# Splitting the first token chunk of an attention front end in two halves, in a fused sketch-attention and MLP kernel on Trainium2

## The chip, the cores and the metric

The kernel runs on one core of one Trainium2 chip. It is timed as device microseconds of one execution, the median of five runs. A second source is one profiled execution, whose trace gives the start and duration of every instruction on the engines: PE (TensorE matmuls), PEld (TensorE weight loads), DVE (VectorE), ACT (ScalarE), POOL (GpSimd), and SP, which here only issues DMAs.

## The reference, cut to what matters

```python
def phi(x):                                   # 32 -> 64 features per token and head
    a = np.einsum('rd,bhsd->bhsr', S1, x)
    b = np.einsum('rd,bhsd->bhsr', S2, x)
    return np.einsum('bhsi,bhsj->bhsij', a, b).reshape(*x.shape[:-1], r * r)
q_p, k_p = (phi(q), phi(k))
kv = np.einsum('bhsf,bhsd->bhfd', k_p, v)
z = np.sum(k_p, axis=2)
num = np.einsum('bhsf,bhfd->bhsd', q_p, kv)
den = np.einsum('bhsf,bhf->bhs', q_p, z)[..., None] + 1e-06
x = num / den                                 # then (B, H, S, D) -> (B*S, H*D)
h = x @ w_in
out = (0.5 * h * (1.0 + erf(h / sqrt(2)))) @ w_out
```

There are 4 batches, 4 heads, 1088 tokens and 32 dimensions per head. `w_in` is 128 x 2048 and `w_out` 2048 x 128. S1, S2, `w_in` and `w_out` arrive as 64-bit floats, and the kernel itself turns them into 32-bit ones; the program calls that "rounding".

## The kernel before, in words

The tokens of each batch are 1024 "main" ones in two chunks of 512 and 64 "remaining" ones. That gives eight main chunks (n = 0 to 7) and a ninth of the remaining tokens of all batches. For each chunk the query features are multiplied with that batch's `kv` and `z`, divided, laid out as `xT` (128 model dimensions by 512 tokens), and fed to 16 hidden tiles (`hidden`, L591: matmul L596, Gelu L603) and their projections (L673 and L724).

Nothing of the MLP can start before batch 0 is summed over its keys and chunk 0 is divided. The text from L757 to L816 is this start, written out by hand. All engines run their instructions in the order of the text, and a dependency ties each instruction to the one before it on its engine (L992 to L998). So the order in the text is the order in each queue.

The start runs as follows. Three matmuls of noughts (`keep_busy`, L755) precede the key transposes (L333). The sketch matrices are transposed (`sketches`, L319). Keys go through the sketch (L375) and become features (L389 and L392); the queries of chunk 0 are expanded (L497, L504, L510). `kv_first` (L432) sums `kv` over eight token blocks for each of two head groups r. The remaining keys of batch 0 go their own way: `key_turn_rem` transposes them (L333 for PE, L335 for the copy on ACT), `key_features_rem` sketches them (L399 on PE, L404 on ACT, L405 on POOL), and `kv_first_rem` (L438) adds them to `kv`. ACT copies the sum out of PSUM as `kz` (L794). The queries of chunk 1 are transposed (L333, copy L796).

Then `attend_by_token` (L552) computes numerators and denominators of chunk 0 with tokens on partitions: 32 small matmuls (L562) into two PSUM banks, one per pair of heads. DVE adds 1e-6 to the denominators (L567, one instruction per bank), takes reciprocals (L568) and multiplies (L570, one per bank) into `x_tok`. `turn_x` (L573) transposes `x_tok` with four matmuls (L578) into two banks, and ACT and DVE copy one half each into `xT` (L581). After a further matmul of noughts (L810) the first hidden tile begins. Between these lie chunk 1's expansion (`expand_products(1)`), and the rounding of the first pieces of the weights: `low_words` L267 and `exponents` L279 on ACT, `fields` L271 and L273, `mantissas` L287 and `signs` L292 on DVE, `product` L297 on POOL or DVE.

The loads of `w_out` piece 0 (L784) and of everything else (`load_rest`, L801) are issued by SP, but each `w_out` load of the first two pieces waits for a one-element write by POOL (L168), which serves as a gate in time.

From L948 the steps are a fixed list: chunk 0 and chunk 1 each take hidden tiles 0 to 3, then the rest follow, with projections two steps behind. In step t = 3 chunk 1 goes through `attend_by_token` as well, and in step 4 through `turn_x`.

PSUM has eight banks here: two for hidden tiles (`h_ps`), two for outputs (`o_ps`), and two pairs for other work (`w_ps`). A pool hands out its buffers in turn, and who gets one waits for the last reader of what it held.

Of the kernel before, what the change touches and what calls it, by code (L numbers as in the profile page):

```python
# [16 lines left out]
def kernel(  # L17
# [49 lines left out]
    def work_banks():  # L67

        return wps.tile([128, 2, CW], FP, name="w_ps")
# [283 lines left out]
    def key_turn(b, r, ps, copy, midway=lambda: None):  # L353
        kT[r] = transposed(ps, "kT", [four_tokens("k", b, h, c) for h in (r, r + 2) for c in range(NCH)], copy, midway)
# [71 lines left out]
    def kv_first(ps, r, tokens=range(J)):  # L426

        for i in tokens:

            ch, t, one = i // 4, i // 2 % 2, i % 2  # L430
            for c in range(NP):
                pe.matmul(ps[c * F:(c + 1) * F, r * 2 * D:(r + 1) * 2 * D], lhsT=flat(k_p[0, r][:, t, c * 4 + ch * 2 + one]),  # L432
                          rhs=v_aug[r][:, c, i, :], start=(r == 0 and i == 0), stop=False, skip_group_check=True)
# [54 lines left out]
    def expand_products(n):  # L488


        W = width[n]
        B_of[n] = [work_banks() for i in range(2)]
        for s in range(2):
            for g in range(G):
                for c in range(NP):
                    rows = slice(g * D, (g + 1) * D)
                    pe.matmul(B_of[n][g // 2][c * F:(c + 1) * F, g % 2, s * W // 2:(s + 1) * W // 2],  # L497
                              lhsT=Srep[rows, s].rearrange("p i j -> p (i j)"),
                              rhs=qT[n][rows, 2 * c:2 * c + 2].rearrange("p r j t -> p r (j t)"), start=True, stop=True)
        qp[n] = att.tile([128, 2, CW], FP, name="q_pT")  # L500

    def expand_copy(n, i):
        A[i] = att.tile([128, 2, CW // 2], FP, name="A_sb")
        act.copy(out=A[i][:, :, :width[n] // 2], in_=B_of[n][i][:, :, :width[n] // 2])  # L504

    def expand_multiply(n, i):
        W = width[n]
        a, b = (t.rearrange("f g (r x) -> f g r x", r=2) for t in (A[i][:, :, :W // 2], B_of[n][i][:, :, W // 2:W]))
        if n < NMAIN:
            dve.tensor_mul(out=qp[n].rearrange("f r (g x) -> f g r x", g=G)[:, 2 * i:2 * i + 2], in0=a, in1=b)  # L510
            return

        cols = qp[n][:, :, :W].rearrange("f r (j g t) -> f g r j t", g=G, t=32)
        a, b = (x.rearrange("f g r (j t) -> f g r j t", t=32) for x in (a, b))
        for g in range(2):
            dve.tensor_mul(out=cols[:, 2 * i + g], in0=a[:, g], in1=b[:, g])
# [32 lines left out]

    x_tok = {}  # L550

    def attend_by_token(n, banks, meanwhile=lambda: None):  # L552

        x_tok[n] = att.tile([128, JC, H, D], FP, name="x_tok", bufs=1)
        den = att.tile([128, NP, JC * 2], FP, name="den_tok")
        for i in range(JC):
            for r in range(2):
                for half in range(2):
                    for c in range(NP):
                        rows, at, tok = slice(c * F, (c + 1) * F), (i * 2 + r) * C, i * 128 + half * 64  # L560
                        v_at = kz_cols(0, 2 * c + r)[0]
                        pe.matmul(banks[c][half * 64:(half + 1) * 64, at:at + C], lhsT=qp[n][rows, r, tok:tok + 64],  # L562
                                  rhs=kz[0][rows, v_at:v_at + C], start=True, stop=True)
        meanwhile()
        nd = [banks[c][:, :JC * 2 * C].rearrange("p (g c) -> p g c", c=C) for c in range(NP)]
        for c in range(NP):
            dve.tensor_scalar(out=den[:, c], in0=nd[c][:, :, D], scalar1=1e-6, scalar2=None, op0=AX.add)  # L567
        dve.reciprocal(out=den, in_=den)  # L568
        for c in range(NP):
            dve.tensor_mul(out=x_tok[n][:, :, 2 * c:2 * c + 2], in0=nd[c][:, :, 0:D].rearrange("p (j r) d -> p j r d", r=2),  # L570
                           in1=den[:, c].rearrange("p (j r) -> p j r", r=2)[:, :, :, None].broadcast_to([128, JC, 2, D]))

    def turn_x(n, banks):  # L573

        xT[n] = att.tile([128, CW], FP, name="xT", bufs=3)
        for i, ps in enumerate(banks):
            for j in range(2):
                pe.transpose(ps[:, j * 128:(j + 1) * 128], in_=x_tok[n][:, 2 * i + j].rearrange("p h d -> p (h d)"),  # L578
                             identity=ident)
        for i, (ps, copy) in enumerate(zip(banks, (by_act, by_dve))):  # L580
            copy(out=xT[n][:, i * 256:(i + 1) * 256], in_=ps[:, :256])  # L581


    g_of, o_of = {}, {}
# [1 line left out]
    def w_tile(w, fi):  # L586
        i = max(i for i, (c0, c1) in enumerate(pieces) if c0 <= fi * 128)
        at = fi * 128 - CUTS[i]
        return w[i][:, at:at + 128]

    def hidden(n, fi, by_halves=False):  # L591
        W = width[n]
        ps = hidden_bank()
        w = w_tile(w_in_sb, fi)
        for rows in (slice(0, 64), slice(64, 128)) if by_halves else (slice(0, 128),):
            pe.matmul(ps[rows, :W], lhsT=w[:, rows], rhs=xT[n][:, :W], start=True, stop=True)  # L596
        if n < NCH and fi < USUAL:
            g_of[n, fi] = mlp.tile([128, CW], FP, name="g", bufs=4)
        else:
            if fi % NB == 0:  # L600
                blocks[n, fi // NB] = block(FP)
            g_of[n, fi] = blocks[n, fi // NB][:, fi % NB]
        act.activation(out=g_of[n, fi][:, :W], in_=ps[:, :W], func=ACT.Gelu)  # L603

# [159 lines left out]
    r.signs()  # L764
    r.product_for_heads(SR_heads)
    key_turn(0, 0, hidden_bank(), by_act)
    sketches()
    key_turn(0, 1, hidden_bank(), by_act)
    query_turn(0)
# [7 lines left out]
    for i in range(2):  # L777
        query_features(0, i)
    kv_bank = out_bank()
    kv_first(kv_bank, 0)  # L780
    key_turn_rem(0, banks[1], by_act)
    kv_first(kv_bank, 1, range(J // 2))
    key_features_rem(0, banks[1], by_pool=True)
    load_w_out(0, gated=True)  # L784
    kv_first(kv_bank, 1, range(J // 2, J))
    kv_first_rem(kv_bank)
    w_in = [Rounding(w) for w in w_in_sb[:2]]
    w_out = [Rounding(w_out_sb[0], beside=w_in[0])]
    w_in[0].low_words()
    w_in[0].fields()  # L790
    w_in[0].exponents()
    late = []
    query_turn(1, lambda **a: late.append(a))
    act.copy(out=kz[0], in_=kv_bank[:, :128])  # L794
    w_in[1].low_words()
    by_act(**late[0])  # L796
    w_in[0].mantissas()
    w_in[0].signs()
    w_in[0].product(pool)
    w_in[1].fields()  # L800
    load_rest()  # L801
    w_out.append(Rounding(w_out_sb[1], beside=w_in[1]))
    w_in[1].exponents()
    banks = [hidden_bank(), hidden_bank()]
    attend_by_token(0, banks)
    expand_products(1)
    w_in[1].mantissas()
    expand_copy(1, 0)
    turn_x(0, [hidden_bank(), hidden_bank()])
    keep_busy(1, out_bank())  # L810
    w_in[1].signs()
    w_in[1].product(pool)
    expand_copy(1, 1)
# [134 lines left out]
    for t in range(len(steps) + LAG):  # L948
        if t < 4:

            hidden(0, t)
            if t == 1:
                w_out[0].exponents()
                w_out[0].low_words()
                w_out[0].finish()
                w_out[1].fields()
            if t == 2:
                w_out[1].low_words()
            if t == 3:
                attend_by_token(1, halves(work_banks()), lambda: (w_out[1].mantissas(by_pool=True),  # L960
                                                                  w_out[1].exponents()))
                w_out[1].signs()
                w_out[1].product()
                for u in range(4):
                    for f, *a in products[u]:
                        f(*a)
            continue
        if t == 4:
            turn_x(1, [work_bank(), work_bank()])
# [59 lines left out]
```

## Time and profile before

| | |
|---|---|
| median of 5 runs | 271.6 us (271.29 to 273.21) |
| the profiled execution's own time | 271.96 us |
| its span, first to last instruction | 270.1 us, so 1.86 us lie around it |
| PE busy | 264.5 us, 98% of the span |
| DVE, ACT, POOL busy | 153.2, 136.6 and 170.3 us |
| first hidden matmul of chunk 0 starts (L596) | 16.86 us |
| steady alternation of hidden tiles and projections | from about 25 us, one hidden tile or projection per 0.86 us |

How to read it: a matmul on 32-bit floats appears as two rows in the trace (four hidden tiles are "x8"), a transpose as one. Ends of matmuls are modelled, so that a stream of matmuls overlaps in the trace: the hidden matmul's row has 592 ns, but in the stream one starts every 430 ns. The view by slices shows PE at nine tenths in all but the first and the last slice; the first slice is 6.75 us wide, so what happens in the start has to be read in the timeline.

### The profile page before, as it was taken

How to read it: one execution, taken by the hardware profiler on the slowest of the kernel's cores; microseconds unless marked ns; L12 is line 12 of the kernel's file. 1: busy time of each engine (PE TensorE's matmuls, PEld its weight loads, DVE VectorE, ACT ScalarE, POOL GpSimd, SP SyncE). 2: the span in 40 equal slices, each digit the busy share in tenths (PEclk: the TensorE clock that was granted, in tenths of full speed). 3: DMA queues.
4: the chain of work that ended last, by engine and by line, in shares of the span. 5: the costliest groups of instructions: out<-in, count | busy, mean ns of one | idle time of the engine just before them, and what ended most of it. 6: DMA issues, size and time to landing. Idle time of an engine off the chain costs nothing.

```text
span 270.1 us, 6237 instructions
## 1 busy us (share of the span) xinstructions
PE 264.5 (98%) x2557; PEld 138.1 (51%) x2557; DVE 153.2 (57%) x242; ACT 136.6 (51%) x272; POOL 170.3 (63%) x178
## 2 busy tenths in 40 slices
PE   8999999999999999999999999999999999999994
PEld 6745445354445545435445445444544544445794
DVE  4856879514793699379214997287018901750140
ACT  4554777456625633573347433663357334733431
POOL 3512006899998498368865896668866886777300
PEclk9999999999999999999999999999999999999998
DMA  7479263626101000110200000100200020011020
GB/s 204 134 231 340 61 165 70 173 60 175 18 0 32 12 0 2 19 22 1 41 1 2 0 2 13 29 2 1 38 2 0 2 40 2 0 21 20 1 42 20
DMA packets 37869, 13.52 MB, mean 50 GB/s; under 512 B 28240, under 2 KB 37200, under 8 KB 37840
## 3 DMA queue, kind: packets, MB, share of 16 engines
q1 hardware_dynamic: 37648, 13.05, 19.1%
q8 instruction: 20, 0.33, 0.5%
q10 hardware_dynamic: 192, 0.07, 0.1%
q14 instruction: 9, 0.07, 0.1%
HBM read 10.88 MB, written 2.23 MB: 49 GB/s over the span
## 4 chain that ended last, share of the span: by engine, by line
PE 97%; DVE 1%; issue 0%; ACT 0%; POOL 0%
PE h_ps L596 44%; PE o_ps L673 32%; PE o_ps L724 5%; PE w_ps L497 3%; PE w_ps L721 3%; PE w_ps L537 2%; PE w_ps L444 2%; PE w_ps L755 1%; PE w_ps L375 1%; PE h_ps L333 1%; PE o_ps L432 1%; PE h_ps L562 0%; PE w_ps L562 0%; PE o_ps L333 0%; DVE x_tok L570 0%
## 5 line engine op out<-in xcount | busy, mean ns | idle before, releaser
L596 PE MATMUL h_ps<-xT,w_in 128*64 128x512 f32 (+3 forms) x518 | 140.8, 577 | 0.2 <-DVE xT L581 0.2
L603 ACT ACTIVATE block<-h_ps 128x512 f32<-128x512 f32 (+1 forms) x128 | 72.8, 571 | 101.6 <-PE h_ps L596 98.5
L673 PE MATMUL o_ps<-block,w_out 128*64 128x256 f32 x224 | 57.9, 381 | 0.0
L596 PEld LDWEIGHTS h_ps<-xT,w_in 128*64 128x64 f32 (+1 forms) x518 | 42.1, 143 | 29.6 <-issue 9.6
L638 POOL TENSOR_TENSOR bits_low<-block 128x512 f32<-128x512 f32 x28 | 36.5, 1303 | 27.7 <-ACT block L603 27.5
L673 PEld LDWEIGHTS o_ps<-block,w_out 128*64 128x64 f32 x224 | 30.0, 137 | 36.9 <-issue 27.6
L639 POOL TENSOR_TENSOR bits_a<-block 128x512 f32<-128x512 f32 x28 | 36.1, 1289 | 15.9 <-ACT block L603 15.6
L641 POOL TENSOR_TENSOR bits_m<-block,bits_e 128x512 f32<-128x512 f32 x28 | 36.3, 1298 | 2.2
L640 POOL TENSOR_TENSOR bits_e<-bits_a,block 128x512 f32<-128x512 f32 x28 | 36.2, 1294 | 2.2
L544 DVE RECIPROCAL den<-den 128x512 f32<-128x512 f32 (+1 forms) x7 | 21.9, 3122 | 14.0 <-ACT den L543 14.0
L673 PE MATMUL o_ps<-bits_a,small 128*64 128x256 f32 x112 | 29.0, 382 | 0.0
L673 PE MATMUL o_ps<-bits_m,w_out 128*64 128x256 f32 x112 | 28.9, 380 | 0.0
L673 PE MATMUL o_ps<-block,small 128*64 128x256 f32 x112 | 28.7, 379 | 0.0
L673 PE MATMUL o_ps<-bits_low,small 128*64 128x256 f32 x112 | 28.7, 379 | 0.0
L510 DVE TENSOR_TENSOR q_pT<-A_sb,w_ps 128x512 f32<-128x512 f32 x16 | 10.3, 682 | 30.2 <-ACT A_sb L504 30.1
L689 DVE TENSOR_TENSOR sums<-o_ps,sums 64x512 f32<-64x512 f32 x8 | 5.5, 682 | 35.9 <-ACT sums L686 20.4
L673 PEld LDWEIGHTS o_ps<-block,small 128*64 128x64 f32 x112 | 15.3, 137 | 18.0 <-issue 12.9
L548 DVE TENSOR_TENSOR xT<-w_ps,den 32x512 f32<-32x512 f32 (+1 forms) x28 | 18.2, 649 | 1.4 <-DVE den L544 0.5
L673 PE MATMUL o_ps<-bits_e,small 128*64 128x256 f32 x112 | 16.8, 379 | 0.0
L724 PE MATMUL o_ps<-g,w_out 128*128 128x512 f32 x32 | 16.4, 599 | 0.1
L543 ACT ACTIVATE den<-w_ps 32x512 f32<-32x512 f32 (+1 forms) x28 | 15.6, 557 | 1.3 <-PE w_ps L537 1.0
L673 PEld LDWEIGHTS o_ps<-bits_low,small 128*64 128x64 f32 x112 | 15.3, 137 | 0.0
(160 smaller groups left out, 314.4 us busy)
## 6 DMA issues: line engine op xcount, KB each, us to landing
block<-in_moe_w_in_dram SPq DMA_DIRECT2D x3, 512.0 KB, 6.3
block<-in_moe_w_out_dram SPq DMA_DIRECT2D x3, 512.0 KB, 9.2
k<-in_k_dram SPq DMA_DIRECT2D x48, 32.0 KB, 1.9
v<-in_v_dram SPq DMA_DIRECT2D x3, 512.0 KB, 4.2
q<-in_q_dram SPq DMA_DIRECT2D x24, 64.0 KB, 3.4
out_dram<-oT SPq DMA_DIRECT2D x24, 64.0 KB, 2.2
k<-in_k_dram SPq DMA_DIRECT2D x2, 256.0 KB, 2.8
q<-in_q_dram SPq DMA_DIRECT2D x2, 256.0 KB, 4.6
```

The lines of the kernel that those rows point to most:

```text
L510: dve.tensor_mul(out=qp[n].rearrange("f r (g x) -> f g r x", g=G)[:, 2 * i:2 * i + 2], in0=a, in1=b)
L543: act.activation(out=den[h * D:(h + 1) * D, :W], in_=banks[h // 2][at:at + D, :W], func=ACT.Copy, bias=1e-6)
L544: dve.reciprocal(out=den[:, :W], in_=den[:, :W])
L548: dve.tensor_mul(out=xT[n][rows, :W], in0=banks[h // 2][at:at + D, :W], in1=den[rows, :W])
L596: pe.matmul(ps[rows, :W], lhsT=w[:, rows], rhs=xT[n][:, :W], start=True, stop=True)
L603: act.activation(out=g_of[n, fi][:, :W], in_=ps[:, :W], func=ACT.Gelu)
L638: pool.tensor_sub(out=s[3], in0=a11, in1=a21)
L639: pool.tensor_add(out=s[1], in0=a21, in1=a22)
L640: pool.tensor_sub(out=s[2], in0=s[1], in1=a11)
L641: pool.tensor_sub(out=s[4], in0=a12, in1=s[2])
L673: pe.matmul(acc[n][bank][half * 64:(half + 1) * 64, col:col + HW], lhsT=fixed, rhs=moving, start=opens and e == 0 and name in "4715", stop ...
L724: pe.matmul(o_of[n], lhsT=w_tile(w_out_sb, fi), rhs=g, start=first, stop=final)
```

## The change

Six edits, all in the start and in what it calls:

1. A small matmul of noughts (128 columns) is put between the first key transposes and the transpose of the sketches.
2. The remaining keys of batch 0 are transposed after the first four of head group 0's token blocks, and sketched before head group 1's blocks. The total of matmuls stays the same.
3. Both gated loads, and with them the gates on POOL, come behind the product of `w_in` piece 0 on POOL. `mantissas` of `w_in` piece 1 on DVE come ahead of chunk 0's division.
4. Chunk 0's numerators go into four banks: tokens of blocks 0 and 1 into the two hidden banks, of blocks 2 and 3 into the two output banks. Chunk 1's expansion follows as before. Then DVE divides one half after the other: two additions, one reciprocal and two multiplications (each of half the size) for each half.
5. Each half of `x` is turned on its own: two transposes and a copy, on DVE for half 0 and on ACT for half 1. The first hidden tile is made of two matmuls of 256 columns, one for each half. The matmul of noughts of L810 is gone.
6. For chunk 1 the two additions of L567 become one over both banks, and the two multiplications of 256 elements become four of 128.

```diff
     key_turn(0, 0, hidden_bank(), by_act)
+    keep_busy(1, bank, 128)
     sketches()
...
-    kv_first(kv_bank, 0)
+    kv_first(kv_bank, 0, range(4))
     key_turn_rem(0, banks[1], by_act)
-    kv_first(kv_bank, 1, range(J // 2))
+    kv_first(kv_bank, 0, range(4, J))
     key_features_rem(0, banks[1], by_pool=True)
-    load_w_out(0, gated=True)
-    kv_first(kv_bank, 1, range(J // 2, J))
+    kv_first(kv_bank, 1)
     kv_first_rem(kv_bank)
...
     act.copy(out=kz[0], in_=kv_bank[:, :128])
-    w_in[1].low_words()
-    by_act(**late[0])
     w_in[0].mantissas()
     w_in[0].signs()
     w_in[0].product(pool)
+    load_w_out(0, gated=True)
+    load_rest()
+    w_out = [Rounding(w, beside=b) for w, b in zip(w_out_sb[:2], w_in)]
+    w_in[1].low_words()
+    by_act(**late[0])
     w_in[1].fields()
-    load_rest()
-    w_out.append(Rounding(w_out_sb[1], beside=w_in[1]))
     w_in[1].exponents()
-    banks = [hidden_bank(), hidden_bank()]
-    attend_by_token(0, banks)
+    w_in[1].mantissas()
+    parts = [range(2), range(2, JC)]
+    nd = [[hidden_bank(), hidden_bank()], [out_bank(), out_bank()]]
+    for banks, tokens in zip(nd, parts):
+        numerators_by_token(0, banks, tokens)
     expand_products(1)
-    w_in[1].mantissas()
+    for banks, tokens in zip(nd, parts):
+        divide(0, banks, tokens, by_head_pair=True)
     expand_copy(1, 0)
-    turn_x(0, [hidden_bank(), hidden_bank()])
-    keep_busy(1, out_bank())
+    turn_half(0, 0, hidden_bank(), by_dve)
+    turn_half(0, 1, hidden_bank(), by_act)
+    for half in range(2):
+        first_hidden(half, range(1))
     w_in[1].signs()
     w_in[1].product(pool)
     expand_copy(1, 1)
...
+    def divide(n, banks, tokens, by_head_pair):
+
+        g = len(tokens) * 2
+        den = att.tile([128, NP, JC * 2], FP, name="den_tok")[:, :, :g]
+        parts = [slice(c, c + 1) for c in range(NP)] if by_head_pair else [slice(0, NP)]
+        nd = [(banks[c.start][:, None] if by_head_pair else banks)[:, :, :g * C].rearrange("p b (g c) -> p b g c", c=C)
+              for c in parts]
+        for c, x in zip(parts, nd):
+            dve.tensor_scalar(out=den[:, c], in0=x[:, :, :, D], scalar1=1e-6, scalar2=None, op0=AX.add)
         dve.reciprocal(out=den, in_=den)
+        for i in range(len(tokens) // 2):
+            to = x_half(n, tokens[0] // 2 + i).rearrange("p j (c r) d -> p c j r d", c=NP)
+            for c, x in zip(parts, nd):
+                for b in range(c.stop - c.start):
+                    dve.tensor_mul(out=to[:, c.start + b], in0=x[:, b, i * 4:i * 4 + 4, 0:D].rearrange("p (j r) d -> p j r d", r=2),
+                                   in1=den[:, c.start + b, i * 4:i * 4 + 4].rearrange("p (j r) -> p j r", r=2)[:, :, :, None]
+                                   .broadcast_to([128, 2, 2, D]))
+
+    def turn_half(n, i, ps, copy):
+        if i == 0:
+            xT[n] = att.tile([128, CW], FP, name="xT", bufs=3)
+        for j in range(2):
+            pe.transpose(ps[:, j * 128:(j + 1) * 128], in_=x_tok[n, i][:, j].rearrange("p h d -> p (h d)"), identity=ident)
+        copy(out=xT[n][:, i * 256:(i + 1) * 256], in_=ps[:, :256])
...
+    def first_hidden(half, fis):
+
+        for fi in fis:
+            if half == 0:
+                first_banks[fi] = hidden_bank()
+            cols = slice(half * 256, (half + 1) * 256)
+            pe.matmul(first_banks[fi][:, cols], lhsT=w_tile(w_in_sb, fi), rhs=xT[0][:, cols], start=True, stop=True)
...
-                attend_by_token(1, halves(work_banks()), lambda: (w_out[1].mantissas(by_pool=True),
-                                                                  w_out[1].exponents()))
+                banks = work_banks()
+                numerators_by_token(1, halves(banks), range(JC))
+                w_out[1].mantissas(by_pool=True)
+                w_out[1].exponents()
+                divide(1, banks, range(JC), by_head_pair=False)
```

`numerators_by_token` is the matmul loop of `attend_by_token` over the given token blocks. `hidden` takes the bank of `first_hidden` and leaves out its own matmul for chunk 0, tile 0. `expand_products` keeps its two pairs of banks, under another name.

More of the change, by code (lines that the diff above doesn't have):

```diff
@@ L491, in expand_products @@
         W = width[n]
-        B_of[n] = [work_banks() for i in range(2)]
+        for i in range(2):
+            B_of[n, i] = work_banks()
         for s in range(2):
@@ L496, in expand_products @@
                     rows = slice(g * D, (g + 1) * D)
-                    pe.matmul(B_of[n][g // 2][c * F:(c + 1) * F, g % 2, s * W // 2:(s + 1) * W // 2],
+                    pe.matmul(B_of[n, g // 2][c * F:(c + 1) * F, g % 2, s * W // 2:(s + 1) * W // 2],
                               lhsT=Srep[rows, s].rearrange("p i j -> p (i j)"),
@@ L503, in expand_copy @@
         A[i] = att.tile([128, 2, CW // 2], FP, name="A_sb")
-        act.copy(out=A[i][:, :, :width[n] // 2], in_=B_of[n][i][:, :, :width[n] // 2])
+        act.copy(out=A[i][:, :, :width[n] // 2], in_=B_of[n, i][:, :, :width[n] // 2])
     def expand_multiply(n, i):
         W = width[n]
-        a, b = (t.rearrange("f g (r x) -> f g r x", r=2) for t in (A[i][:, :, :W // 2], B_of[n][i][:, :, W // 2:W]))
+        a, b = (t.rearrange("f g (r x) -> f g r x", r=2) for t in (A[i][:, :, :W // 2], B_of[n, i][:, :, W // 2:W]))
         if n < NMAIN:
@@ L550, with numerators_by_token @@
     x_tok = {}
[L552 to L556, printed above, removed]
+    def numerators_by_token(n, banks, tokens):
+        for at, i in enumerate(tokens):
             for r in range(2):
@@ L559, in attend_by_token @@
                     for c in range(NP):
-                        rows, at, tok = slice(c * F, (c + 1) * F), (i * 2 + r) * C, i * 128 + half * 64
+                        rows, col, tok = slice(c * F, (c + 1) * F), (at * 2 + r) * C, i * 128 + half * 64
                         v_at = kz_cols(0, 2 * c + r)[0]
-                        pe.matmul(banks[c][half * 64:(half + 1) * 64, at:at + C], lhsT=qp[n][rows, r, tok:tok + 64],
+                        pe.matmul(banks[c][half * 64:(half + 1) * 64, col:col + C], lhsT=qp[n][rows, r, tok:tok + 64],
@@ L563, in attend_by_token @@
                                   rhs=kz[0][rows, v_at:v_at + C], start=True, stop=True)
[L564 to L581, printed above, removed]
+    def x_half(n, i):
+        x_tok[n, i] = att.tile([128, 2, H, D], FP, name=f"x_tok{i}", bufs=1)
+        return x_tok[n, i]
@@ L589, in w_tile @@
         return w[i][:, at:at + 128]
+    first_banks, begun = {}, [(0, 0)]
     def hidden(n, fi, by_halves=False):
         W = width[n]
-        ps = hidden_bank()
+        ps = first_banks.pop(fi) if fi in first_banks else hidden_bank()
         w = w_tile(w_in_sb, fi)
         for rows in (slice(0, 64), slice(64, 128)) if by_halves else (slice(0, 128),):
-            pe.matmul(ps[rows, :W], lhsT=w[:, rows], rhs=xT[n][:, :W], start=True, stop=True)
+            if (n, fi) not in begun:
+                pe.matmul(ps[rows, :W], lhsT=w[:, rows], rhs=xT[n][:, :W], start=True, stop=True)
         if n < NCH and fi < USUAL:
@@ L779 @@
     kv_bank = out_bank()
-    kv_first(kv_bank, 0)
+    kv_first(kv_bank, 0, range(4))
     key_turn_rem(0, banks[1], by_act)
-    kv_first(kv_bank, 1, range(J // 2))
+    kv_first(kv_bank, 0, range(4, J))
     key_features_rem(0, banks[1], by_pool=True)
-    load_w_out(0, gated=True)
-    kv_first(kv_bank, 1, range(J // 2, J))
+    kv_first(kv_bank, 1)
     kv_first_rem(kv_bank)
     w_in = [Rounding(w) for w in w_in_sb[:2]]
-    w_out = [Rounding(w_out_sb[0], beside=w_in[0])]
     w_in[0].low_words()
@@ L968 @@
         if t == 4:
-            turn_x(1, [work_bank(), work_bank()])
+            for i, copy in enumerate((by_act, by_dve)):
+                turn_half(1, i, work_bank(), copy)
             for f, *a in products[t]:
```

## The prediction

> **What bounds the kernel now.** I read the page's busy table and chain first, then the chain of the first 45 us in order of time, and last the timelines of DVE and ACT from 8 to 18 us.
>
> From the page (chain by engine):
>
> ```profile
> PE 97%; DVE 1%; issue 0%; ACT 0%; POOL 0%
> ```
>
> PE carries 97% of the path. From about 25 us a hidden tile or a projection starts every 0.86 us without a gap, and no edit touches what PE does there. So the end moves by as much as PE's arrival in that stream moves, and only the start can give or take anything. The chain in order of time, where it leaves PE:
>
> ```profile
> 10.02 0.62 PE o_ps L432 x16
> 10.63 0.38 PE o_ps L399 x2
> 11.01 0.02 issue
> 11.04 0.22 ACT a_rem L404
> 11.26 0.07 issue
> 11.33 0.62 POOL k_p_rem L405
> ...
> 12.01 0.45 PE o_ps L438 x8
> 12.46 0.59 PE o_ps L333 x4
> 13.04 1.14 PE h_ps L562 x64
> 14.18 0.23 DVE den_tok L567 x2
> 14.41 0.02 issue
> 14.44 0.27 DVE den_tok L568
> 14.70 0.02 issue
> 14.72 0.77 DVE x_tok L570 x2
> 15.49 0.14 issue
> 15.63 0.64 PE h_ps L578 x4
> 16.27 0.02 issue
> 16.29 0.43 DVE xT L581
> ```
>
> Two places leave PE with nothing that it may do. The first is the detour of the remaining keys, L399 to L438, 1.38 us long and covered by only half of head group 1 (0.55 us in the weight-load row): PE is idle 0.39 us before L438. The second runs from the numerators to the first hidden tile: division 1.31 us, transposes, copy. Chunk 1's expansion (1.12 us) covers part of it. Two more lines, from the timelines of DVE and of ACT, matter below:
>
> ```profile
> 12.69 0.84 DVE L273 TENSOR_SCALAR bits_a<-small 128x256 uint32<-128x256 uint32 x1
> 13.08 0.59 ACT L796 COPY qT<-o_ps 128x512 f32<-128x512 f32 x1
> ```
>
> The first is a 0.28 us instruction that took 0.84 us while POOL multiplied w_in piece 0 (12.65 to 13.38). The second is what the new output banks have to wait for.
>
> **The change part by part.** Times are those of the profiled execution (271.96 us; span 270.1 plus 1.86 around it). It lies 0.36 above the median of 271.6; I carry the difference over to the median.
>
> *The small matmul of noughts.* It is one matmul of 128 columns, two rows. Before it PE is idle from about 4.49 (last transpose started at 4.28, one every 0.21) to 4.72, when L319 starts as SR_heads is ready. Transposes of 128 columns start 0.21 to 0.23 us apart here, so two rows take 0.46 from 4.49: L319 slips to 4.95, by 0.23. The next transposes follow at once, so the copy of kT and the second L375 slip by about 0.2. The expansion L497 does so by less: at 7.44 it waited for qT on DVE (7.29, and DVE to PE takes about 0.14 in these rows), which does not move, since it hangs on q's DMA. Of PE's delay 0.12 is left. Bounds: 0, if the rows overlap more, and 0.46. I take 0.12, because qT's row is the nearest cover.
>
> *The remaining keys.* In front of L399 lie 16 fewer rows of L432 (0.55 us of weight loads), behind it 16 more. So L399 can start 0.55 earlier, at 10.01, if kT_rem is copied: ACT is free at 9.66 (end of the two L504), copies 0.27, and PE takes it at about 10.0. Fits. From L399 the detour needs 1.38 to L438, while PE now has 0.37 (L399) and 1.04 (32 rows) to do: the idle 0.39 to 0.53 (PE, weight-load row) is filled. Gain 0.5, minus the 0.12 above: L438 starts at about 11.63 instead of 12.01. k_rem's second DMA was issued at 4.2 and took 4.7, so it lands at about 8.9; the transpose now comes at 9.4. Half a microsecond of cover; if it were gone, each tenth would cost a tenth.
>
> *Gates and loads.* The two one-element writes on POOL move behind the product (0.73 us), so w_out piece 0 is issued at about 13.1 instead of 12.01. It lands 2.9 us later (DMA view), at 16.0, and DVE reads it at about 17.4. SP's queue behind it stays: what held it was the second gate (13.57), which now comes slightly earlier, so w_in piece 2, needed after 23 us, isn't late. Cost nothing, as long as the 1.4 us of cover hold.
>
> *Mantissas ahead of the division.* 0.42 us of DVE, which lay after x_tok (15.39), now stands before it. With L438 at 11.63, kz is copied by 12.4 and the first numerators start at 12.6 (12.97 before); half of them (32 rows, 0.53 and the latency) can be read at 13.2. DVE: signs end at 12.15, fields with the slow L273 at 13.05 (POOL's product moves along), mantissas at 13.47. So the division starts at 13.47, 0.27 later than its data.
>
> *Numerators in four banks.* The second half needs the output bank that held chunk 1's queries until L796 has copied them: 13.67 before, about 13.25 now. PE is through with half 0 at 13.13, so it waits 0.1 to 0.2. Behind it stand the expansion and the transposes, and it ends at about 15.0, before the division does. Not on the path.
>
> *Division by halves.* Rows: L567 0.16 us each and 0.23 the pair, L568 0.25, L570 0.42 each and 0.77 the pair. There is no row for 128 elements; the product of 64 elements out of PSUM (L320) took 0.225, so by a straight line 128 take 0.29, and a pair about 0.50. One half: 0.23 + 0.03 + 0.22 + 0.03 + 0.50 = 1.0; both 2.0 instead of 1.31. [...] The rows make it 0.7 and 15.47. I take the rows. [...]
>
> *Transposes, copies, first tile.* What follows the last x before: 0.14 + 0.64 + 0.02 + 0.43 + 0.14, to 16.86. Now only half 1 comes after it: 0.14, two transposes 0.43 (0.64 less two starts of 0.107), 0.03, ACT's copy 0.37, and about 0.1 to PE: 16.54. Half 0 was turned behind the expansion at 15.0 to 15.35, copied by DVE after the division (15.5 to 15.9), and its 256 columns run at 16.05 to 16.48. So at 16.54 only half 1's 0.43 is left, and hidden tile 1 starts at 16.97. Before it started at 16.86 + 0.86 = 17.72. Gain 0.75.
>
> *After that.* Gelu 0 is earlier by as much, so hidden tile 2, whose bank waits for it, keeps its distance (it lost 0.1 before and may lose less). w_in piece 1: signs follow half 0's copy, product on POOL to about 17.0, wanted at 17.8. Chunk 1's division: one addition instead of two (-0.1), four products of 128 for two of 256 (about 0.93 for 0.77), so x is 0.06 to 0.15 later; it is hidden behind two projections (x at 23.15, transposes at 23.51), but w_out piece 1's product, which stands behind it on DVE and ends at 24.02 right before the projection at 24.17, slips too. Cost 0 to 0.15; I take 0.05.
>
> Sum: -0.75 + 0.05 = -0.7; 271.96 becomes 271.26, and the median 271.6 becomes 270.9.
>
> **The clock.** The removed matmul of noughts filled part of the gap before hidden tile 1. The row first: matmuls of noughts took 634 ns at the start and 382 at 16 us, though the granted clock reads 1.00 in both windows; transposes 421 and 272. So there is a slow state that the clock row does not show, and it ended near 5.7 us. [...] By the rows, a fall would make the following hidden tiles about twice as long.
>
> **The rivals.**
>
> *The division takes all of it.* For: by my sum DVE has hardly any idle time between 11.6 and 16; the 0.84 row shows that POOL can triple an instruction; the small matmul may cost up to 0.46. With 0.3 more on DVE and 0.25 more from the matmul, x is complete at 15.9 and the gain is 0.1 to 0.3: 271.4. Against: these are outer values of both. Chance 0.2.
>
> *More than I sum.* [...] Chance 0.1.
>
> *Slower: the clock falls.* In place: between 13 and 16.5 us, with the matmul of noughts gone, and small numerators and transposes as PE's only work besides the expansion. [...] Against it: PE's busy share was 1.03 of 1.5 us at 14.5 to 16 before, without a fall, and the idle total gets smaller. Chance 0.1.
>
> **How the numbers follow.** My forecast has 0.6: 270.9, by itself 270.4 to 271.3 (0.25 each way for the small matmul, 0.2 for the division, 0.1 for chunk 1). Range 270.2 to 271.8: it takes in the first rival and most of the second, and leaves out the slow one. A measurement of this kernel tells about 0.5% (1.36 us) from no change. Faster by more than that, under 270.24: most of the second rival, 0.1. Slower by more, over 272.96: most of the third, 0.08. Within it: 0.82.
>
> **What would show it.** Right: no idle PE before L438, which starts near 11.6; first products of the two halves of x near 14.0 and 15.0, the last ending at 15.3 to 15.6; hidden tile 1 at about 17.0; the stream from 25 us on unchanged but 0.7 earlier. Wrong: hidden matmuls of 800 ns or more after 16 us (the clock); L399 waiting for kT_rem; a last x after 15.8; DVE waiting for w_out piece 0 near 17.4; or an early shift that is given back at the projection of w_out piece 1.

## The result, and the profile after

The changed kernel takes 271.18 us (median of 43 executions, 270.65 to 274.19); the kernel before, measured again beside it, 271.65 (80 executions, 271.25 to 274.75). The medians are 0.47 us apart. The means, 272.03 before and 271.33 after, are 0.70 apart, and the ratio of the two kernels over all executions agrees with them: 0.9974, interval 0.9963 to 0.9986, which is 0.7 us less, within 0.4 to 1.0. The profiled execution took 271.20 us against 271.96, with a span of 269.4 against 270.1.

The forecast was 270.9 with a range of 270.2 to 271.8, a gain of 0.7. First the chain of work that ended last, of the changed kernel, from the sketch of the remaining keys to hidden tile 1 (start, duration, what):

```profile
10.19 0.38 PE o_ps L399 x2
10.57 0.02 issue
10.59 0.21 ACT a_rem L404
10.80 0.37 ACT bits_low L267
11.17 0.02 issue
11.19 0.60 DVE bits_m L287
11.79 0.34 DVE bits_e L292
12.12 0.20 DVE bits_e L271
12.33 0.77 DVE bits_a L273
...
13.19 0.43 DVE bits_m L287
13.62 0.15 DVE den_tok L576 x2
...
14.03 0.49 DVE x_tok L582 x2
...
14.92 0.50 DVE x_tok L582 x2
15.43 0.14 issue
15.56 0.41 PE h_ps L590 x2
15.97 1.16 PE h_ps L624 x4
17.13 0.87 PE h_ps L609 x2
```

The detour over POOL (L405) and the stop before L438 are gone from the chain. In their place DVE's rounding of `w_in` carries it, from 11.19 up to the division: after L399 the chain no longer runs through the end of the `kv` sum and its copy. The division's first addition starts as soon as the mantissas (13.19, ahead of it now) have ended. After the last product of x only two transposes, their copy and half of the first tile remain. (The chain counts a piece from the end of the piece ahead, so hidden tile 1 stands at 17.13 there; its row in the timeline starts at 16.97.) The instruction that takes three times its usual 0.28 us beside POOL's product (12.20 to 12.93) is there as before, in the timeline of DVE:

```profile
12.25 0.84 DVE L273 TENSOR_SCALAR bits_a<-small 128x256 uint32<-128x256 uint32 x1
```

Set beside the sum: L438 starts at 11.56 (forecast 11.63), the numerators at 12.53 (12.6), the division at 13.53 (13.47), the two halves of x end at 14.52 and 15.41 (14.47 and 15.47), hidden tile 1 starts at 16.97 (16.97). PE in the timeline of the changed kernel, from tile 0 on:

```profile
15.97 1.17 PE L624 MATMUL h_ps<-xT,w_in 128*128 128x256 f32 x4
16.97 2.90 PE L609 MATMUL h_ps<-xT,w_in 128*128 128x512 f32 x6
```

In the trace of the kernel before, the second row of tile 0 starts at 17.37, 0.51 us after the first (16.86) and not 0.43, so that hidden tile 1 starts at 17.80. It is 0.83 earlier now, 0.08 more than the 0.75 of the sum, which had it at 17.72. Projection (0, 2), with `w_out` piece 1, starts at 23.45 against 24.17: 0.72 earlier (0.7). So 0.11 of the shift is given back there (0.05 in the sum): PE waits 0.17 for DVE's product of `w_out` (L297).

### The profile page after: what moved, and what is told of

Same layout as the page of the kernel before. It is cut to its first block, busy times and chain, and to the rows that moved or that the text cites. A ratio compares the mean times of both kernels' runs of the same rounds, so it can differ in the third digit from the quotient of the medians.

```text
span 269.4 us, 6251 instructions
## 1 busy us (share of the span) xinstructions
PE 264.7 (98%) x2559; PEld 138.7 (51%) x2559; DVE 154.4 (57%) x248; ACT 136.5 (51%) x272; POOL 170.1 (63%) x178
## 4 chain that ended last, share of the span: by engine, by line
PE 94%; DVE 3%; ACT 1%; issue 0%; DVEq 0%; ACTq 0%
PE h_ps L609 43%; PE o_ps L694 32%; PE o_ps L745 5%; PE w_ps L498 3%; PE w_ps L742 3%; PE w_ps L538 3%; PE w_ps L444 2%; PE w_ps L776 1%; PE w_ps L375 1%; PE h_ps L333 1%; DVE x_tok L582 1%; DVE bits_m L287 1%; PE o_ps L432 0%; PE h_ps L624 0%; DVE bits_e L292 0%
## 6 DMA issues: line engine op xcount, KB each, us to landing
k<-in_k_dram SPq DMA_DIRECT2D x2, 256.0 KB, 2.8
q<-in_q_dram SPq DMA_DIRECT2D x2, 256.0 KB, 4.0
```

## The experiments

Each is measured beside the kernel before on one chip, though not all on the same one. Executions over 272.3 us are counted apart as "long", because the times of most of these kernels fall into two heaps with a gap between them (for the kernel before none lies between 272.14 and 273); what the long ones are comes below. "Usual" is the median of the others. The ratios leave out one execution of over 275 us each in e2, e5 and e7.

| kernel | usual, us | kernel before beside it, usual | ratio (interval) | long |
|---|---|---|---|---|
| changed kernel | 271.11 | 271.56 | 0.9974 (0.9963 to 0.9986) | 5 of 43 |
| changed kernel, again (e11) | 271.26 | 271.47 | 0.9976 (0.9955 to 0.9997) | 1 of 14 |
| e1, only the remaining keys moved | 271.09 | 271.57 | 0.9987 (0.9962 to 1.0012) | 4 of 14 |
| e2, no small matmul of noughts | 270.99 | 271.57 | 0.9969 (0.9950 to 0.9989) | 5 of 22 |
| e3, mantissas late | 270.97 | 271.57 | 0.9969 (0.9955 to 0.9984) | 1 of 21 |
| e4, remaining keys back | 271.40 | 271.57 | 0.9986 (0.9967 to 1.0004) | 3 of 21 |
| e5, whole division | 271.01 | 271.61 | 0.9954 (0.9930 to 0.9977) | 4 of 22 |
| e6, whole first tile | 271.51 | 271.61 | 0.9989 (0.9963 to 1.0015) | 3 of 14 |
| e7, turn amid expansion | 271.35 | 271.61 | 0.9971 (0.9948 to 0.9994) | 4 of 22 |
| e8, two noughts at the start | none | 271.61 | 1.0037 (1.0015 to 1.0059) | 22 of 22 |
| e9, gap filled too | 271.23 | 271.47 | 0.9973 (0.9957 to 0.9989) | 0 of 22 |
| e10, four noughts at the start | 271.07 | 271.47 | 0.9981 (0.9967 to 0.9995) | 0 of 22 |
| e12, mantissas late and gap filled | 271.24 | 271.56 | 0.9972 (0.9956 to 0.9988) | 0 of 22 |

The two measurements of the changed kernel differ by 0.15 in the usual time. So 0.2 between two measurements is no difference, and the parts are better told from the traces, by lengths within one trace. Two stretches do it: A from the first matmul of chunk 0's expansion (L497, L498 after) to the first of chunk 0's numerators, B from there to hidden tile 1 (where tile 0 is one matmul of 512 columns, 0.93 us after its first row). In e7's trace the slow phase at the start lasts so long (to 17.1 us) that its A is left out; its B is taken up below.

| | before | changed | e1 | e3 | e4 | e5 | e6 | e7 |
|---|---|---|---|---|---|---|---|---|
| A, us | 5.53 | 4.99 | 5.00 | 4.99 | 5.47 | 5.08 | 5.01 | - |
| B, us | 4.82 | 4.44 | 4.82 | 4.37 | 4.44 | 4.54 | 4.88 | 4.62 |

**e1: only the remaining keys moved.** The kernel before with

```diff
-    kv_first(kv_bank, 0)
+    kv_first(kv_bank, 0, range(4))
     key_turn_rem(0, banks[1], by_act)
-    kv_first(kv_bank, 1, range(J // 2))
+    kv_first(kv_bank, 0, range(4, J))
     key_features_rem(0, banks[1], by_pool=True)
     load_w_out(0, gated=True)
-    kv_first(kv_bank, 1, range(J // 2, J))
+    kv_first(kv_bank, 1)
```

> The kernel before with only the remaining keys moved amid kv (the second edit), everything else as before. My theory (the gain is the filled wait before L438 plus half 1's shorter way after the last x): L399 starts near 10.0 and L438 near 11.5 instead of 12.01, the division follows at 13.65 and the first hidden tile at 16.35 instead of 16.86, so 0.5 us less than before (ratio 0.998). The rival that the halves give the gain and the remaining keys only move a wait along: L438 is earlier but the first hidden tile stays within 0.1 of 16.86, ratio 1.000.

PE in the timeline of e1 (start, duration, then what ended the idle time, if there was any):

```profile
11.42 0.45 PE L438 MATMUL o_ps<-v_rem_aug,k_p_rem 128*64 128x64 f32 x8
12.39 1.14 PE L562 MATMUL h_ps<-kz,q_pT 64*64 64x33 f32 x64
16.27 3.83 PE L596 MATMUL h_ps<-xT,w_in 128*128 128x512 f32 x8 [0.17 <-DVE xT L581]
```

L438 has no idle time before it, and the first tile starts at 16.27 instead of 16.86. A is 0.53 shorter and B as before. The usual time is 0.48 lower, the ratio's interval includes 1. My theory, not the rival's: the remaining keys are worth about half a microsecond by themselves. In usual times that is already as much as the whole change gains (0.46); the account at the end comes back to it.

**e4: the reverse,** the changed kernel with those lines as they were.

> The changed kernel with the remaining keys where they were before. My theory: L438 goes back to 12.1, and with it kz, numerators and division: 0.5 us more than the changed kernel, so 0.2 us less than before. The rival that DVE's rounding (fields, mantissas, done at 13.6) bounds the division whatever kv does: 0.2 us more or less than the changed kernel.

PE in the timeline of e4:

```profile
11.59 0.45 PE L438 MATMUL o_ps<-v_rem_aug,k_p_rem 128*64 128x64 f32 x8 [0.39 <-POOL k_p_rem L405]
12.56 0.67 PE L561 MATMUL h_ps<-kz,q_pT 64*64 64x33 f32 x32
```

The idle 0.39 is back, to the digit. A is 0.48 longer and B equal to that of the changed kernel, as my theory has it. The usual time is 0.29 above that of the changed kernel, between the theory's 0.5 and the rival's 0.2, so the time alone would not decide. DVE's rounding moved along with the kv sum, since `low_words` on ACT stands behind the copy of `a_rem` there; so the rival's fixed DVE does not hold either.

**e6: the first tile whole.** The changed kernel without `first_hidden`; hidden tile 0 is one matmul of 512 columns.

```diff
-    for half in range(2):
-        first_hidden(half, range(1))
...
-    first_banks, begun = {}, [(0, 0)]
+    first_banks, begun = {}, []
```

> The changed kernel with the first hidden tile as one matmul of 512 columns behind both halves of xT; numerators, division and turning by halves stay. My theory: the tile starts when half 1 is copied, and all of its 0.86 us comes after that instead of 0.43: hidden tile 1 comes 0.4 us later than in the changed kernel, and the time is 0.4 us longer. The rival that the stretch is bound by what follows (rounding of w_in piece 1, Gelu): within 0.1 of the changed kernel.

```profile
15.44 0.41 PE L590 MATMUL h_ps<-ident,x_tok 128*128 128x128 f32 x2 [0.20 <-DVE x_tok L582]
16.36 3.83 PE L609 MATMUL h_ps<-xT,w_in 128*128 128x512 f32 x8 [0.51 <-ACT xT L591]
```

PE stands idle for 0.51 us until ACT has copied half 1, which the 256 columns of half 0 filled in the changed kernel. B is 0.44 longer, the usual time 0.4 above the changed kernel's. As expected.

**e5: the division whole.** Numerators in two banks, one division of all tokens; half 0 and half 1 are still turned apart.

```diff
-    parts = [range(2), range(2, JC)]
-    nd = [[hidden_bank(), hidden_bank()], [out_bank(), out_bank()]]
+    parts = [range(JC)]
+    nd = [[hidden_bank(), hidden_bank()]]
```

> The changed kernel with chunk 0's numerators in two banks and one division of all tokens, as before; turning and first tile by halves stay. My theory (the gain of the halves comes from turning and first tile, the split division costs DVE as much as it hides): from the start of the first L498 to hidden tile 1, 9.43 us in the changed kernel, it stays within 0.1, and so does the time. The rival that the halved numerators and x are what gains: 0.4 us or more above the changed kernel.

DVE in the timeline of e5:

```profile
13.88 0.24 DVE L576 TENSOR_SCALAR den_tok<-h_ps 128x8 f32<-128x8 f32 x2
14.15 0.25 DVE L577 RECIPROCAL den_tok<-den_tok 128x16 f32<-128x16 f32 x1
14.44 0.88 DVE L582 TENSOR_TENSOR x_tok<-h_ps,den_tok 128x128 f32<-128x128 f32 x4
15.72 0.42 DVE L591 COPY xT<-h_ps 128x256 f32<-128x256 f32 x1 [0.40 <-PE h_ps L590]
```

One division takes 1.44 us (13.88 to 15.32) where two take 1.88 (13.53 to 15.41), but the first transposes start at 15.28 only, as their bank holds numerators until the third product. From the first L498 to hidden tile 1 it is 9.61 instead of 9.43, more than the 0.1 of my theory; but 0.08 of that arises ahead of the numerators, which this edit does not touch. B is 0.10 longer, and the usual time 0.10 shorter: far from the rival's 0.4. Four banks and halved numerators, the words by which one would name this change, are worth about a tenth of a microsecond at most.

**e3: mantissas late.** In the changed kernel,

```diff
     w_in[1].exponents()
-    w_in[1].mantissas()
...
         first_hidden(half, range(1))
+    w_in[1].mantissas()
     w_in[1].signs()
```

> The changed kernel with the mantissas of w_in piece 1 behind DVE's copy of half 0, instead of ahead of the division. My theory (DVE from the slow L273 to the last x is the bound): the division starts at 13.2, when half 0's numerators are there, instead of 13.53, the last x ends near 15.1 instead of 15.41, and hidden tile 1 starts near 16.7 instead of 16.97: 0.25 to 0.3 us less than the changed kernel. The rival that PE bounds this stretch (half 1's numerators wait for L822, then expansion and transposes): no change against the changed kernel within 0.1.

DVE, then PE, in the timeline of e3:

```profile
12.68 0.23 DVE L576 TENSOR_SCALAR den_tok<-h_ps 128x4 f32<-128x4 f32 x2 [0.17 <-PE h_ps L561]
14.82 0.42 DVE L591 COPY xT<-h_ps 128x256 f32<-128x256 f32 x1 [0.25 <-PE h_ps L590]
```

```profile
14.35 0.78 PE L590 MATMUL h_ps<-ident,x_tok 128*128 128x128 f32 x4
15.39 1.10 PE L624 MATMUL h_ps<-xT,w_in 128*128 128x256 f32 x4 [0.27 <-DVE xT L591]
```

Here my theory failed. The division did start with its data (0.72 after the numerators instead of 1.00) and the last x was 0.27 earlier, as expected. But both pairs of transposes now stand in one piece behind the expansion, DVE waits 0.25 for half 0's transposes, and B shrinks by 0.07 only. The rival was right: behind DVE, PE's expansion is the next bound, less than a tenth away.

**e7: half 0 turned amid the expansion,** on top of e3, with both copies on ACT.

```diff
-    expand_products(1)
     for banks, tokens in zip(nd, parts):
         divide(0, banks, tokens, by_head_pair=True)
+    expand_products(1, lambda: turn_half(0, 0, hidden_bank(), by_act))
     expand_copy(1, 0)
-    turn_half(0, 0, hidden_bank(), by_dve)
     turn_half(0, 1, hidden_bank(), by_act)
```

> The kernel with late mantissas, and half 0's two transposes in the middle of chunk 1's expansion, both copies of xT on ACT. The late mantissas alone brought x 0.27 forward, but hidden tile 1 only 0.07 (9.36 after the first L498), since half 0's transposes waited for the end of the expansion. My theory now: PE's order is the bound there; half 0 is copied before the expansion ends, its 256 columns run at 8.0 to 8.4, half 1's at 8.65 to 9.1 after the first L498, so hidden tile 1 is at 9.1: 0.3 us less than the changed kernel, about 0.8 less than before. The rival that something else stands next (copies on ACT behind exponents and A_sb, or w_in piece 1): at 9.3 or later, within 0.1 of the kernel with late mantissas.

The profiled execution is a long one (275.54 us), and its first numerators still ran slowly: with the same instructions the division starts 0.91 us after the first numerator where e3 takes 0.72. From there on its matmuls have their usual durations, so B may be read less about 0.19. PE, then ACT, in its timeline:

```profile
16.64 0.86 PE L563 MATMUL h_ps<-kz,q_pT 64*64 64x33 f32 x32
```

```profile
19.14 0.37 ACT L593 COPY xT<-h_ps 128x256 f32<-128x256 f32 x1 [1.40 <-PE h_ps L592]
19.81 0.58 ACT L507 COPY A_sb<-w_ps 128x512 f32<-128x512 f32 x1 [0.30 <-PE w_ps L500]
20.30 0.38 ACT L593 COPY xT<-h_ps 128x256 f32<-128x256 f32 x1
```

The copy of half 0 starts 2.5 us after the first numerators instead of 2.9 (e3). Half 1's copy, however, stands in ACT's queue behind the copy of A_sb, and its 256 columns start at 20.73, 4.09 after the numerators. B is 4.62, or about 4.43 without the slow numerators: no better than the 4.37 of e3. The usual time is 0.38 above that of e3. The rival named the place.

**e2: no small matmul of noughts.**

```diff
     key_turn(0, 0, hidden_bank(), by_act)
-    keep_busy(1, bank, 128)
     sketches()
```

> The changed kernel without the small matmul of noughts between key transposes and sketch transpose. My theory: the matmul only costs, about 0.1 us on the path, so the usual time is 0.1 us less than that of the changed kernel (0.7 to 0.8 below before). The rival that it matters for TensorE's slow state at the start: the usual time is hardly touched, but the share of executions that take about 1.8 us longer, 5 of 43 for the changed kernel and 20 of 80 for the one before, goes back to about a quarter.

The usual time is 0.12 lower, which is what I took for the matmul, though no more than two measurements of one kernel may differ. The share of long executions, 5 of 22, is near that of the kernel before (85 of 292), as the rival has it. By itself it proves little: 22 executions can't tell it from the 21 of 157 with the small matmul (changed twice, e3 to e7), and the times of e2 have no gap at 272.3 (272.22 lies below, 272.33 above). But 21 of 157 and 85 of 292 are clearly apart, and the other edits of these kernels act only after 8.6 us, later than the slow phase at the start lasts in most traces (to 6.3 us at most in twelve of fourteen). That made me look for what the long executions are.

**e8: two matmuls of noughts at the start instead of three.**

```diff
-    keep_busy(3, bank)
+    keep_busy(2, bank)
```

> The changed kernel with two instead of three matmuls of noughts at the very start, so that PE idles about 0.9 us before the first key transposes. Theory that TensorE leaves its slow state only after a window that is busy enough: the share of executions about 1.8 us longer (9 of 85 with the small matmul so far, against about 28% without it) rises to a third or more, or all executions become longer. The rival that the long executions have another cause (a late load): the share stays near a tenth, and the usual time as it is.

PE in the timeline of e8:

```profile
3.63 1.09 PE L333 MATMUL h_ps<-ident,k 128*128 128x128 f32 x4 [0.81 <-DMA k<-in_k_dram]
8.19 2.01 PE L498 MATMUL w_ps<-qT,Srep 32*64 32x256 f32 x32
13.49 0.66 PE L333 MATMUL o_ps<-ident,q 128*128 128x128 f32 x4
```

The expansion takes 2.01 us, in the changed kernel's trace 1.12; later the same kinds of matmul have their usual length. All 22 executions are long, at 272.6 or more. So in this kernel TensorE stays in its half-rate phase until past 10 us instead of until 3.6 to 6.3 us. (Half, because in the traces of the kernel before and of the changed one the transposes start 0.213 us apart in that phase and 0.109 us apart later.) Leaving out one matmul of noughts, so that PE is idle for 0.81 us before the keys have landed, is enough to cause it every time. That it takes a busy window to end the phase was my guess: the run shows the idle time and the longer phase, not what ends it. Its profiled execution takes 1.6 us more than that of the changed kernel, which is about how far the heaps lie apart. I take the long executions of the other kernels to be of the same kind; of these only one was traced, e7's, and there the phase lasts still longer.

The record of the granted clock in each trace says the same as the durations. It has no entry at the start, which the view by windows counts as 1.00; its first stretch, at full clock, begins where the durations drop, and ends at most 1.6 us before the end of the span:

| | e2 | e4 | e10 | e3 | e11 | e6 | before | e5 | changed, e1, e12 | e9 | e8 | e7 |
|---|---|---|---|---|---|---|---|---|---|---|---|---|
| full clock from, us | 3.61 | 3.64 | 4.11 | 4.69 | 4.91 | 5.63 | 5.79 | 5.95 | 5.98 to 5.99 | 6.30 | 10.27 | 17.10 |

The "long" 272.31 of e5 is the traced one, so it is of another kind: it lost 0.8 us after 24 us. All these stretches at full clock last 256.0 (e7), 259.4 (e8), 262.8 (before and changed among others) or 266.2 us: they differ by 3.4 us, or by two or three times as much. A half-rate phase that is 3.4 us longer would cost 1.7 us (an estimate from these lengths and from the distances of the transposes, 0.213 and 0.109 us); the usual heap of the kernel before lies around 271.6, the next around 273.3. At the start, gaps of a few tenths of a microsecond on PE decided here: 0.81 us in e8, where every execution is long, and at most 0.3 us in the gap that e9 fills, where none is.

**e9 and e10: no gap at all.**

```diff
     keep_busy(3, bank)
+    keep_busy(1, bank, 64)
```

in e9; `keep_busy(4, bank)` in e10.

> The changed kernel with a further matmul of noughts, 64 columns, behind the first three, in the gap before the first key transposes (from about 3.5 to 3.6 or 3.7 in the traces). [...] Theory: with this gap filled too, the share of long executions falls below a twentieth (20 of 143 with the small matmul so far, 77 of 250 without it); the usual time is 0 to 0.2 us longer than the changed kernel's. The rival that this gap is too short to count, or the long executions have a second cause: the share stays at a seventh.

> The changed kernel with four instead of three matmuls of noughts at the start: they last until about 4.4, past the landing of the keys at 3.5, so PE never idles before the key transposes, which start 0.8 us later. Theory: no long executions beyond chance; the usual time is 0.4 to 0.8 us longer than the changed kernel's where the slow state ends late, less where it ends within the noughts. The rival (a second cause): long executions at a seventh as before.

> The changed kernel itself, once more, beside the two others: 0.46 us below the kernel before as in its first measurement, within 0.15; long executions at about a seventh. It bounds what the comparisons of kernels from different calls are worth.

PE in the timeline of e9, where the noughts now last until the keys:

```profile
0.77 3.22 PE L776 MATMUL w_ps<-const-float32-0.0 128*128 128x256 f32 x8 [0.77 <-PEq L1045]
3.79 1.06 PE L333 MATMUL h_ps<-ident,k 128*128 128x128 f32 x4
```

With e12 there are no long executions in 66, where a share of 21 in 157 would give nine. Filling the gap is what does it. Whether the idle time counts, or the amount of matmul work in that time, no run tells: each of these edits changes both. e10's usual time was expected to be 0.4 to 0.8 longer where the half-rate phase ends late. Its median is not longer than the changed kernel's (271.07 and 271.11), but the times spread widely (270.56 to 272.17). That the upper ones have a late end is not shown; the one trace has an early end.

The second measurement of the changed kernel (e11) missed its expectation: its usual time is 0.21 below the kernel before, not 0.46 within 0.15. Its share of long ones, 1 of 14, fits. PE in its timeline:

```profile
3.58 1.08 PE L333 MATMUL h_ps<-ident,k 128*128 128x128 f32 x4
7.08 1.12 PE L498 MATMUL w_ps<-qT,Srep 32*64 32x256 f32 x32
```

This execution took 270.80 us, with full clock from 4.91, and the first traced one of the same kernel 271.20, with full clock from 5.98. A and B are alike (5.00 and 4.46 here); the 0.4 lies between the first key transpose and the expansion, 3.50 us here and 3.91 there. So with an earlier or later full clock the time of one kernel moves by 0.4 us, more than half of what the change gains.

**e12: late mantissas and the gap filled.**

> The changed kernel with the late mantissas and the further matmul of noughts of 64 columns, the two edits that looked best. Theory: no long executions (0 of 44 with the gap filled), and hidden tile 1 about 4.37 after the first numerators instead of 4.44, so a median of 271.0 to 271.2, at or a little below the changed kernel, and a mean over all executions some 0.2 below the changed kernel's. The rival that the late mantissas' lower time was a matter of the calls: median as the changed kernel's with the gap filled (271.23).

B is 4.38 and the median 271.24, against 271.23 for e9, as the rival has it: the 0.07 can't be told in the time. Its mean over all executions, 271.21, lies below the changed kernel's 271.33 of the first measurement and equals the 271.20 of the second. So no version was found that clearly beats the changed kernel.

## Why the prediction was right, point by point

*The bound.* Right: the stream from 25 us on starts earlier and is otherwise the same. From projection (0, 2) to the end of the span it is 245.9 us in both.

*Remaining keys, 0.5.* Right, by two experiments: 0.53 alone (e1), 0.48 undone (e4). It is the larger part of the gain.

*Halves.* The total was right (B 0.38 shorter), and so was the place: what comes after the last x. Undoing the halved tile alone loses all of it (0.44). The divided division is even: 0.44 us dearer on DVE for two than for one of the same small products (e5), and hidden. By my line through two rows it was to be 0.7 dearer than the division of the kernel before; measured were 1.88 against 1.32, so 0.56. The error made no difference in time: x ended 0.06 earlier than summed, and the way from there to hidden tile 1 took 0.06 longer.

*Mantissas, 0.27.* The delay of the division was as forecast, but it cost much less than its length: taking it away gains 0.07, since PE's expansion is the next bound (e3).

*The small matmul, 0.12.* Right in the traces of both kernels, in which full clock comes late: the way from the first key transpose to the expansion is 3.91 instead of 3.83 (0.08), although L319 slipped by 0.35 (4.72 to 5.08) and not 0.23. Where full clock comes early the rows show no more. L319 can start 0.33 us after its product L302 on DVE starts (before: 4.39 and 4.72; e2: 4.13 and 4.46). With the small matmul in front it starts 0.15 us later than that in e3, 0.08 in e11 and no later in e4. The way of e2, 3.09 us against 3.42 (e3) and 3.50 (e11), is shorter because its clock was full at 3.61, at the first transposes: four of them take 0.68 us there and 1.08 in the others. The matmul also has a benefit that I gave no number: with it the share of long executions is less than half (29% against 13%).

*So the sum was right partly by luck.* In the traces a gain of 0.08 too little at hidden tile 1 and a cost of 0.06 too little at the projection cancel. In the times, the mean over all executions fell by 0.70 (272.03 to 271.33), but about 0.45 of it is in the usual ones and the other 0.25 comes from fewer long ones, which the forecast had at nothing. (In the second measurement the means are 0.72 apart, the usual times 0.21.) The trace's 0.72 is that of an execution with a late full clock in both kernels. Why the usual ones gain 0.27 less than that, and no more than e1 alone does, isn't settled. One reason may be that the heap itself changes: an execution that is kept from being long becomes a usual one, and perhaps one of the slowest, with full clock late. It would fit that two kernels without long executions have higher usual times, e9 by 0.12 over the changed kernel and e12 by 0.27 over e3; e10, 0.04 below the changed kernel, does not fit, and no run tests it. Late loads may be another, shown by one trace only, that of e2, in PE's timeline:

```profile
11.97 0.63 PE L333 MATMUL o_ps<-ident,q 128*128 128x128 f32 x4 [0.88 <-DMA q<-in_q_dram]
```

PE had finished with kv at 11.1 there and waited for chunk 1's queries, so that a shorter detour brought nothing.

*The rivals.* The division did not take the gain (e5), more than 0.8 wasn't there (e3, e7), and the clock did not fall between 13 and 17 us in any trace: once it was full it stayed so to the last 1.6 us of the span or longer, and hidden matmuls kept 592 ns (the median in the traces of before and changed). My clock rival looked at the right state in the wrong place. What a fall of the clock costs, which the range leaves out, no run shows, nor the larger gain that it takes in: the lowest usual time is e3's 270.97, and a longer half-rate phase was measured at the start alone, where the traced execution took 1.6 us more (e8).

## What to carry to other kernels

Look for the wait that PE has in front of an accumulation's last contribution, and start that contribution's detour earlier: moving two lines in the order gave 0.5 us, more than splitting the stage behind it (0.38). In a split stage it is the part after the last datum that counts (two transposes and half a tile instead of four and a whole), not the stage's own length; and before taking the bound away, see which queue is next behind it. Compare lengths inside a trace when the executions of one kernel scatter by more than the effect, and count the heaps of times before taking medians: an edit can gain by moving executions from one heap to the other.

## What the hardware showed that I had not expected

TensorE's half-rate phase at the start lasts until 3.6 to 6.3 us in the twelve traces that are not long by it, and until 10.3 us in e8. By the times, taking the long executions for such ones, it lasts longer in 29% of the executions of the kernel before, in 13% with a gap of 0.23 us filled, in none of 66 with the second gap filled too (at most 0.3 us, from 3.47, where a seventh row of noughts could start, to the first key transpose), and in 22 of 22 with a gap of 0.81 us. The view of the granted clock reads 1.00 at the start all the same: the durations show the phase (transposes 421 ns against 272, the expansion 2.01 us against 1.12), and so does the start of the first stretch in the clock record. In the longest profiled execution (e7) it lasted to 17.1 us, and that execution took 4 us more than the usual ones of its kernel.
